# k of chunk 2 by 32x32 block loads and VectorE transposes, with the attention of chunks 2 to 5 placed 4 to 6 tiles later

## The chip, the cores and the metric

One core of a Trainium2 chip. The metric is the device time of one execution in microseconds (us). Lines such as L265 are lines of the kernel before; in the changed kernel the helpers stand at the same lines.

## The reference, cut to what matters

A decayed linear attention (a state of 64x64 a head) over 768 positions, then a feed-forward network with a tanh gelu.

```python
def _attn_ref(q, k, v):            # 4 batches, 8 heads, 768 positions, 64 wide
    gamma = 1.0 - 2.0 ** (-5.0 - np.arange(H))
    for t in range(S):
        state = gamma[None, :, None, None] * state + np.einsum('bhd,bhe->bhde', k[:, :, t], v[:, :, t])
        y[:, :, t] = scale * np.einsum('bhd,bhde->bhe', q[:, :, t], state)

def _moe_ref(x, w_in, w_out):      # 3072 tokens, 512 -> 2048 -> 512
    h = x @ w_in
    g = 0.5 * h * (1.0 + np.tanh(c * (h + 0.044715 * h * h * h)))
    return g @ w_out
```

## The kernel before

The positions are cut into six chunks of 128 (0 to 5). For each chunk c, M1 is `h = x @ w_in` with gelu and M2 is `g @ w_out`, 16 tiles each, on TensorE. The attention of chunk c+1 is strewn between those tiles: `att_T` gets q and k transposed, `att_AY` makes the score products A = k q (a pair of batches at a time), `att_Y` the outputs y, `att_S` the new state. TensorE's matmuls stand in the program's order, so the place of each piece is written down by tile number (a tile of 512 columns is four matmuls, 0.86 us).

A transposed operand comes in one of two ways. Either TensorE transposes it into PSUM and an engine copies it out, or it is loaded as 32x32 blocks, GpSimd scales it, and VectorE transposes the blocks within SBUF:

```python
    BLK = {"q": (2, 3, 4, 5), "k": (3, 4, 5)}       # the chunks that take the second way

    def load_blk(nm, c):                            # 16 DMAs of 64 KB, rows of 128 B
        t = ld_all((nm + ("32" if nm == "q" else "T32"), c))
        ...
                    nc.sync.dma_start(out=t[p0:p0 + 32, :, a, :], in_=src[j, dd, t0:t0 + 32])

    def mm_T(c, b):                                 # TensorE, into one of 4 "att" banks of PSUM
        parts = [(i, nm) for i, nm in enumerate("qk") if c not in BLK[nm]]
        ...
                nc.tensor.transpose(out=ps[:, i, hp], in_=pair(h16[nm, c, b], hp), identity=iden)

    def ev_T(c, b, eng=nc.vector):
        for i, nm in enumerate("qk"):
            if c in BLK[nm]:
                nc.vector.transpose(out=t[:, i]..., in_=blk16.pop((nm, c, b))...)
        if ("T", c, b) in pss:
            copy_on(eng, t[:, i0:], pss.pop(("T", c, b))[:, i0:])

    def att_AY(c, bs, tag, ca, abs_, eng):
        ...
        for b in abs_:
            mm_A(ca, b)                             # L265: 8 matmuls a batch, two "att" banks
        ...
            for b in abs_:
                ev_A(ca, b)                         # L278: VectorE, two instructions a batch
```

The schedule around M1 and M2 of chunk 1, and that of the later chunks (n is the next chunk; M1 has units 0 to 15, M2 has 16 to 31):

```python
    for b in range(B):
        load1(SY, "k", 2, b)                        # plain load of k, 256 KB
    load_blk("q", 2)
    ...                                             # three late output stores, v of chunk 2
    run(M1 of chunk 1, {...
            8: [(att_T, 2, 0), (load, 3)], 10: [(att_T, 2, 1)],
            13: [(att_AY, 2, (), "att", 2, (0, 1), None)],
            14: [(att_T, 2, 2)], 15: [(att_T, 2, 3)]})
    run(M2 of chunk 1, {1: [(att_AY, 2, (), "att", 2, (2, 3), None)], 4: [(att_Y, 2)], ...})
    for c in range(2, NCk - 1):
        after = {2: [prep q and k blocks], 6: [(att_T, n, 0)], 8: [(att_T, n, 1)] + [...],
            9: [(load, n + 1)], 10: [(att_T, n, 2)],
            12: [(att_AY, n, (), "att", n, (0, 1), None)], 14: [(att_T, n, 3)],
            17: [(att_AY, n, (), "att", n, (2, 3), None)], 21: [(att_Y, n)], 23 to 26: att_S}
```

## Time and profile before

| | kernel before |
|---|---|
| time, median of 3 runs | 213.74 us (213.71 to 213.85) |
| span of the profiled run | 212.4 us, granted clock 0.998 |
| TensorE busy | 97% |
| chain that ended last | 87% TensorE |
| DMA | 32.78 MB in 124289 packets, 118064 of them under 512 B |

TensorE is the bound nearly everywhere. The useful reading is by stage: from the first h_ps matmul of one chunk's M1 to that of the next one's. A stage holds M1 and M2 of one chunk with the attention of the next, and I name it after the attention in it ("the stage of chunk 3" is M1 and M2 of chunk 2). The lines on which the forecast rests stand in it below.

### The profile page before, as it was taken

The numbers are of one execution on the slowest core, as the hardware profiler recorded it, in microseconds if no ns is written. First come the engines' busy times: TensorE is split into PE (matmuls) and PEld (weight loads), VectorE is DVE, ScalarE is ACT, GpSimd is POOL, SyncE is SP. The second block draws the span as 40 slices with busy tenths as digits, with TensorE's granted clock in tenths as the row PEclk, the third lists the DMA queues.
The fourth block names the chain that finished last, engine by engine and source line by source line (L and its number), as shares of the span: only waits on it lengthen the run. The fifth ranks groups of instructions, "written<-read, shape, count | busy, mean of one in ns | idle before, by whom it ended". The sixth has DMA issues, their size and how long they took to land.

```text
span 212.4 us, 3868 instructions
## 1 busy us (share of the span) xinstructions
PE 205.6 (97%) x1516; PEld 111.3 (52%) x1516; DVE 89.2 (42%) x161; ACT 84.2 (40%) x141; POOL 95.8 (45%) x117
## 2 busy tenths in 40 slices
PE   7989999999999999999999999999999999999992
PEld 2457444457897564444464444464444464444461
DVE  5478201198619753365544365544355520100001
ACT  2374661255455131465131465131465131565110
POOL 2796400513819418599309599301599301100000
PEclk9999999999999999999999999999999999999999
DMA  6999999999789788979789996879910012100121
GB/s 157 288 250 207 206 203 233 241 241 231 127 222 224 112 161 159 252 177 175 120 162 190 303 192 103 124 153 241 281 34 3 0 49 102 49 0 0 49 92 59
DMA packets 124289, 32.78 MB, mean 154 GB/s; under 512 B 118064, under 2 KB 122416, under 8 KB 124272
## 3 DMA queue, kind: packets, MB, share of 16 engines
q1 hardware_dynamic: 108880, 20.75, 49.4%
q0 software_dynamic: 5600, 8.65, 17.2%
q10 hardware_dynamic: 9792, 3.15, 6.1%
q8 instruction: 12, 0.20, 0.4%
q14 instruction: 5, 0.04, 0.1%
HBM read 30.44 MB, written 6.29 MB: 173 GB/s over the span
## 4 chain that ended last, share of the span: by engine, by line
PE 87%; SPq 4%; DVE 2%; DMA 2%; ACT 1%; issue 1%; POOL 0%; POOLq 0%
PE o_ps L470 39%; PE h_ps L425 34%; SPq L110 4%; PE spin_ps L171 4%; PE a_ps L265 3%; PE y_ps L300 3%; PE y_ps L287 2%; DMA q<-in_q_dram 2%; PE s_ps L319 2%; PE qkT_ps L242 2%; ACT qkT L224 1%; DVE qkT L226 1%; DVE qkT L251 1%; POOL q L206 0%; DVE q L195 0%
## 5 line engine op out<-in xcount | busy, mean ns | idle before, releaser
L470 PE MATMUL o_ps<-w_out,g 128*128 128x512 f16 (+1 forms) x400 | 88.1, 371 | 0.0
L425 PE MATMUL h_ps<-xT,w_in 128*128 128x512 f16 (+1 forms) x464 | 86.8, 342 | 0.3 <-ACT g L440 0.2
L440 ACT ACTIVATE g<-h_ps 128x512 f16<-128x512 f32 x96 | 57.2, 597 | 47.8 <-PE h_ps L425 47.8
L425 PEld LDWEIGHTS <-w_in 128*128 128x128 f16 x464 | 44.4, 98 | 37.9 <-issue 0.3
L470 PEld LDWEIGHTS <-g 128*128 128x128 f16 x400 | 37.7, 98 | 38.8
L278 DVE TENSOR_TENSOR a_sb<-a_ps,mask 128x512 f16<-128x512 f32 x48 | 30.0, 682 | 15.9 <-PE a_ps L265 15.8
L492 ACT COPY o_sb<-o_ps 128x512 f32<-128x512 f32 x19 | 11.1, 586 | 54.3 <-PE o_ps L470 49.9
L497 POOL DMA_DIRECT2D out_dram<-o_sb x17 | 9.6, 564 | 46.9 <-ACT o_sb L492 35.0
L195 POOL TENSOR_TENSOR k<-k,cst 128x512 f16<-128x512 f32 x24 | 24.7, 1036 | 11.9 <-DMA k<-in_k_dram 11.8
L345 POOL TENSOR_TENSOR stg<-st,cst 128x512 f32<-128x512 f16 x16 | 16.3, 1041 | 11.5 <-DVE st L336 9.5
L206 POOL TENSOR_TENSOR q<-q,cst 128x512 f16<-128x512 f32 x16 | 16.6, 1048 | 5.2 <-DMA q<-in_q_dram 5.1
L336 DVE TENSOR_TENSOR st<-s_ps,stg 64x256 f16<-64x256 f32 x32 | 13.5, 422 | 7.8 <-PE s_ps L319 7.3
L251 DVE STREAM_TRANSPOSE qkT<-q 128x512 f16<-128x512 f16 x16 | 11.3, 706 | 11.7 <-POOL q L206 11.7
L195 DVE TENSOR_TENSOR q<-q,cst 128x512 f16<-128x512 f32 x8 | 6.3, 781 | 17.2 <-DMA q<-in_q_dram 17.2
L206 POOL TENSOR_TENSOR kT<-kT,cst 128x512 f16<-128x512 f32 x12 | 12.5, 1044 | 0.0
L226 DVE CAST xT<-y_ps 128x512 f16<-128x512 f32 x11 | 7.2, 686 | 11.9 <-PE y_ps L300 11.9
L508 DVE COPY o_sb<-o_ps 128x256 f32<-128x256 f32 x2 | 0.8, 424 | 26.6 <-PE o_ps L470 26.6
L224 ACT CAST xT<-y_ps 128x512 f16<-128x512 f32 x13 | 7.2, 588 | 9.9 <-PE y_ps L300 9.9
L171 PE MATMUL spin_ps<-zero 128*128 128x512 f16 x28 | 9.6, 499 | 1.3 <-DVE zero L139 1.3
L490 DVE COPY o_sb<-o_ps 128x512 f32<-128x512 f32 x4 | 2.8, 691 | 19.0 <-PE o_ps L470 14.7
L265 PE MATMUL a_ps<-qkT 64*128 64x128 f16 x192 | 8.3, 218 | 1.3 <-ACT qkT L224 0.7
L251 DVE STREAM_TRANSPOSE qkT<-kT 128x512 f16<-128x512 f16 x12 | 8.4, 700 | 2.6 <-POOL kT L206 2.6
(32 smaller groups left out, 98.2 us busy)
## 6 DMA issues: line engine op xcount, KB each, us to landing
v<-in_v_dram SPq DMA_DIRECT2D x22, 256.0 KB, 4.4
k<-in_k_dram SPq DMA_DIRECT2D x20, 256.0 KB, 4.9
out_dram<-o_sb POOLq DMA_DIRECT2D x17, 256.0 KB, 3.2
q<-in_q_dram SPq DMA_DIRECT2D x64, 64.0 KB, 2.7
kT<-in_k_dram SPq DMA_DIRECT2D x48, 64.0 KB, 2.7
w_out<-in_moe_w_out_dram POOLq DMA_DIRECT2D x4, 512.0 KB, 15.5
w_in<-in_moe_w_in_dram POOLq DMA_DIRECT2D x3, 512.0 KB, 8.9
q<-in_q_dram SPq DMA_DIRECT2D x5, 256.0 KB, 6.1
```

Source lines behind the costliest of these rows:

```text
L171: nc.tensor.matmul(out=ps, lhsT=zero[:, 0:128], rhs=zero, start=True, stop=True)
L195: eng.tensor_tensor(out=t, in0=src, in1=cst[:, col:col + H].unsqueeze(2).broadcast_to([128, H, Dh]), op=ALU.mult,)
L206: nc.gpsimd.tensor_tensor(out=t, in0=ld_all((key, c))[:, b * NHP:(b + 1) * NHP].rearrange("p hp a d -> p (hp a) d"), in1=cst[:, col:col + ...
L251: nc.vector.transpose(out=t[:, i].rearrange("p hp t -> p (hp t)"), in_=blk16.pop((nm, c, b)).rearrange("p ha d -> p (ha d)"),)
L265: nc.tensor.matmul(out=ps[j][:, hp], lhsT=t[j * 64:(j + 1) * 64, 1, hp], rhs=t[j * 64:(j + 1) * 64, 0, hp], start=True, stop=True,)
L278: nc.vector.tensor_tensor(out=s, in0=ps[j], in1=mask[:, j], op=ALU.mult)
L336: eng.tensor_tensor(out=st[sl, :, b, sl], in0=s_ps[sl, :, sl], in1=stg[sl, :, b, sl], op=ALU.add,)
L345: nc.gpsimd.tensor_tensor(out=stg[:, :, b], in0=st[:, :, b], in1=cst[:, OG:OG + NHP].unsqueeze(2).broadcast_to([128, NHP, 128]), op=ALU.mult,)
L425: nc.tensor.matmul(out=out, lhsT=w_in_of(fc, kc), rhs=xT[c][:, kc, t0:t1], start=(kc == 0 and first), stop=(kc == NHP - 1), skip_group_che ...
L440: nc.scalar.activation(out=out, in_=in_, func=AF.Gelu_apprx_tanh, scale=1.0)
L470: nc.tensor.matmul(out=ps[:, n0:n1], lhsT=g_sb[c, fc // 2][:, fc % 2, b * C:(b + 1) * C], rhs=w_out_sb[fc // (NF // NO)][:, fc % (NF // NO ...
L492: nc.scalar.copy(out=o_sb, in_=ps)
```

## The change

Its intent: k of chunk 2 also takes the block way, so TensorE loses 16 transposes of 128x128. Since these blocks arrive later, the attention moves back in all later stages. Plain k is still loaded, as the state product needs it.

```diff
-    BLK = {"q": (2, 3, 4, 5), "k": (3, 4, 5)}
+    BLK = {"q": (2, 3, 4, 5), "k": (2, 3, 4, 5)}
...
-    for b in range(B):
-        load1(SY, "k", 2, b)
     load_blk("q", 2)
+    load_blk("k", 2)
     for rows, o_sb in late: ...
-    (v of chunk 2; preps of k, q, v of chunk 2 at once)
+    (v, then k of chunk 2); load(3); prep(2, "Q")
...  M1 of chunk 1
-            8: [(att_T, 2, 0), (load, 3)], 10: [(att_T, 2, 1)],
-            13: [(att_AY, 2, (), "att", 2, (0, 1), None)],
-            14: [(att_T, 2, 2)], 15: [(att_T, 2, 3)],
+            7: [(prep, 2, "Kvk")],
...  M2 of chunk 1
-            1: [(att_AY, 2, (), "att", 2, (2, 3), None)], 4: [(att_Y, 2)], 6 to 9: att_S
+            1: [(att_T, 2, 0), (att_T, 2, 1)],
+            3: [(att_AY, 2, (), "att", 2, (0, 1), None), (att_T, 2, 2), (att_T, 2, 3)],
+            7: [(att_AY, 2, (), "att", 2, (2, 3), None)], 11: [(att_Y, 2)], 12 to 15: att_S
...  chunks 3 to 5
+            2: [(prep, n, "QKvk")],
-            6: T0, 8: T1, 10: T2, 12: A(0,1), 14: T3, 17: A(2,3), 21: Y, 23 to 26: S
+            14: T0, T1, 17: A(0,1), T2, T3, 22: A(2,3), 26: Y, 27 to 30: S
```

(The last two lines are shortened; T, A, Y and S stand for att_T, att_AY, att_Y and att_S.)

More of the change, by code (lines that the diff above doesn't have):

```diff
@@ L634, with prep @@
     )
-    for b in range(B):
-        load1(SY, "k", 2, b)
     load_blk("q", 2)
+    load_blk("k", 2)
     for rows, o_sb in late:
         nc.sync.dma_start(out=rows, in_=o_sb)
-    for b in range(B):
-        load1(SY, "v", 2, b)
-    for nm in "kqv":
+    for nm in "vk":
         for b in range(B):
-            prep_blk("q", 2, b) if nm == "q" else prep1(PO, nm, 2, b)
+            load1(SY, nm, 2, b)
+    load(3)
+    def prep(c, nms):
+        for nm in nms:
+            for b in range(B):
+                prep1(PO, nm, c, b) if nm in "kv" else prep_blk(nm.lower(), c, b)
+    prep(2, "Q")
     run(
@@ L657 @@
             6: [(att_S, 1, 3)],
-            8: [(att_T, 2, 0), (load, 3)],
-            10: [(att_T, 2, 1)],
-            13: [(att_AY, 2, (), "att", 2, (0, 1), None)],
-            14: [(att_T, 2, 2)],
-            15: [(att_T, 2, 3)],
+            7: [(prep, 2, "Kvk")],
         },
@@ L667 @@
         {
-            1: [(att_AY, 2, (), "att", 2, (2, 3), None)],
-            4: [(att_Y, 2)],
-            6: [(att_S, 2, 0)],
-            7: [(att_S, 2, 1)],
-            8: [(att_S, 2, 2)],
-            9: [(att_S, 2, 3)],
+            1: [(att_T, 2, 0), (att_T, 2, 1)],
+            3: [(att_AY, 2, (), "att", 2, (0, 1), None), (att_T, 2, 2), (att_T, 2, 3)],
+            7: [(att_AY, 2, (), "att", 2, (2, 3), None)],
+            11: [(att_Y, 2)],
+            12: [(att_S, 2, 0)],
+            13: [(att_S, 2, 1)],
+            14: [(att_S, 2, 2)],
+            15: [(att_S, 2, 3)],
         },
@@ L680 @@
         after = {
-            2: [(prep_blk, nm, n, b) for b in range(B) for nm in "qk"],
-            6: [(att_T, n, 0)],
-            8: [(att_T, n, 1)] + [(prep1, PO, nm, n, b) for b in range(B) for nm in "kv"],
+            2: [(prep, n, "QKvk")],
             9: [(load, n + 1)] if n + 1 < NCk else [],
-            10: [(att_T, n, 2)],
-            12: [(att_AY, n, (), "att", n, (0, 1), None)],
-            14: [(att_T, n, 3)],
-            17: [(att_AY, n, (), "att", n, (2, 3), None)],
-            21: [(att_Y, n)],
-            23: [(att_S, n, 0)],
-            24: [(att_S, n, 1)],
-            25: [(att_S, n, 2)],
-            26: [(att_S, n, 3)],
+            14: [(att_T, n, 0), (att_T, n, 1)],
+            17: [(att_AY, n, (), "att", n, (0, 1), None), (att_T, n, 2), (att_T, n, 3)],
+            22: [(att_AY, n, (), "att", n, (2, 3), None)],
+            26: [(att_Y, n)],
+            27: [(att_S, n, 0)],
+            28: [(att_S, n, 1)],
+            29: [(att_S, n, 2)],
+            30: [(att_S, n, 3)],
         }
```

## The prediction

> **What bounds the kernel now.** I read the share of each engine first, then the chain that ended last, then the timelines of single engines in the two kinds of stage that the change touches. The page's first part:
>
> ```profile
> PE 205.6 (97%) x1516; PEld 111.3 (52%) x1516; DVE 89.2 (42%) x161; ACT 84.2 (40%) x141; POOL 95.8 (45%) x117
> ```
>
> TensorE is busy for 97% of a 212.4 us span (the timed median, 213.74 us, is 1.3 us more), and the chain is 87% TensorE. Of the 6.8 us without a matmul, about 1.3 lie before the first and 3.8 after the last. So only two things can move the time: matmul work taken off TensorE, and waits of TensorE in the middle. The view of TensorE's waits holds only one of those in the part that the change touches, 0.30 us at 66 us. It is the end of this chain (start, us, what):
>
> ```profile
> 58.22 0.49 SPq L110
> 58.70 0.04 issue
> 58.75 3.79 DMA q<-in_q_dram
> ...
> 62.93 1.06 POOL q L206
> 63.99 0.02 issue
> 64.02 0.72 DVE qkT L251
> 64.74 0.02 issue
> 64.76 0.42 DVE qkT L226
> 65.18 0.62 DVE qkT L251
> 65.80 0.32 DVE qkT L226
> 66.12 0.05 issue
> 66.17 0.40 PE a_ps L265 x8
> 66.56 0.98 PE h_ps L425 x8
> 67.54 0.22 PE qkT_ps L242 x4
> ```
>
> The q blocks of chunk 2 land at 62.54, GpSimd scales them, VectorE transposes them, and the A product of the second batch (L265) stands until 66.17. Eight such matmuls take 0.33 us where nothing is missing; the first of the pair began at 65.47, so 0.37 us is lost. The last line is one of four groups of k transposes, 0.22 us each.
>
> In chunks 3 to 5 there is no such wait: the times from one chunk's first h_ps to the next one's are 31.86, 31.85 and 30.96 us (the last stage has no state products), all TensorE.
>
> **What the Trainium skill says.** "TensorE: Matmul & The Clock Gate", Part 4, gives about 275 to 390 ns for a 128x128 transpose and says that the result goes to PSUM and needs a copy. The copy agrees (L226, 0.38 to 0.42 us); the time doesn't apply here: in a stream four take 0.22 us, 56 ns each, and I use that. "VectorE: DVE Perf Modes", The three transpose paths, says that VectorE transposes 32x32 blocks only, which is why k has to arrive as blocks; in the trace one of 128x512 takes 0.70 us. "DMA: Bandwidth & Descriptors", Specifications, asks for 512 B or more a transfer for line rate; the block loads move 128 B rows, and agree: 64 KB each 0.53 us, 124 GB/s. "SBUF — State Buffer", Who interferes with whom, says that a VectorE instruction with one SBUF input doesn't contend with GpSimd outside the two-port modes; transposes last 0.71 us beside busy GpSimd, so I add nothing for the longer GpSimd work.
>
> **The change, part by part.** *Removed:* 16 transposes of k on TensorE, 4 x 0.22 = 0.9 us on the bound engine, and the four 0.4 us copies on VectorE. *Added:* four VectorE transposes of 0.70 (net +1.2 us), four GpSimd scalings of 1.04 (+4.2 us) and 16 DMAs of 64 KB, since k is still loaded plainly too. All of that lies beside TensorE; in itself it costs nothing. *Moved:* the q wait of 0.37 us goes, as q now heads the queue. So the change is worth -1.26 us if the new order makes no waits.
>
> I find two places where it does. First, arrival. The DMA queue of before:
>
> ```profile
> 44.87 3.66 SPq L98 DMA_DIRECT2D k<-in_k_dram  x4
> 48.62 10.62 SPq L110 DMA_DIRECT2D q<-in_q_dram  x16
> 59.33 2.31 SPq L641 DMA_DIRECT2D out_dram<-o_sb  x3
> ```
>
> In the new order the q blocks start at 44.9, end 10.6 later at 55.5, and the k blocks follow, 9.5 us (their time for chunk 3 in before): 65.0. The last lands 2.8 to 3.8 later, at 67.8 to 68.8. GpSimd can then scale batch 0 and 1 (2 x 1.04, plus 0.3 for its wait on eight semaphores), VectorE ends the second transpose 0.75 after that: 70.9 to 71.9. When does TensorE ask? The last half of M1 loses the four k groups (0.9) and the first A pair with its wait (1.03), so M2 of chunk 1 starts at 68.70 - 1.93 = 66.77, not 68.70. The pair of A products stands after four tiles of 0.864: batch 0 at 70.2, batch 1 at 70.5. Batch 1 waits 0.4 to 1.4, I take 0.9 us.
>
> Second, VectorE between the A pairs. The program order that I built has, on VectorE: four evictions of A(0,1), then all four transposes of batches 2 and 3, then A(2,3) on TensorE. In before only one batch's transposes stood behind the evictions. VectorE, then TensorE, of chunk 3 in before:
>
> ```profile
> 97.83 2.48 DVE L278 TENSOR_TENSOR a_sb<-a_ps,mask 128x512 f16<-128x512 f32 x4 [3.13 <-PE a_ps L265]
> 100.23 0.70 DVE L251 STREAM_TRANSPOSE qkT<-q 128x512 f16<-128x512 f16 x1
> 100.86 0.67 DVE L251 STREAM_TRANSPOSE qkT<-kT 128x512 f16<-128x512 f16 x1
> ```
>
> ```profile
> 97.40 0.62 PE L265 MATMUL a_ps<-qkT 64*128 64x128 f16 x16
> 97.95 2.76 PE L425 MATMUL h_ps<-xT,w_in 128*128 128x512 f16 x12
> 100.55 1.89 PE L470 MATMUL o_ps<-w_out,g 128*128 128x512 f16 x8
> 102.38 0.62 PE L265 MATMUL a_ps<-qkT 64*128 64x128 f16 x16
> ```
>
> From the start of the first pair, evictions begin after 0.43 and take 2.40; the transposes start 0.63 apart, so four end at 0.43 + 2.40 + 3 x 0.63 + 0.70 = 5.42. Batch 3 is asked for after five tiles between the pairs, which is 4.98, plus 0.28 for batch 2: 5.26. With the hand-over of 0.05 that is a wait of 0.2 us in each of chunks 3, 4 and 5: 0.6. For chunk 2 only four tiles lie between the pairs: 4.98 - 0.86 + 0.28 = 4.4 against 5.47. If batch 1 waited there, A and evictions shift together and 1.0 remains.
>
> Sum: -0.9 - 0.37 + 0.9 + 1.0 + 0.6 = +1.2 us, which makes 214.9.
>
> The rest I checked for room and let stand. kT16 has two buffers, so GpSimd's scaling of batches 2 and 3 waits for the first two transposes, but they come before the evictions in VectorE's order. Chunk 2's v and k land by 79, while the first state product is asked for at about 82.7. The next chunk's blocks arrive some 8 us later than before, k's of chunk 3 at 95.5 and scaled by 99.8, and its first A pair now stands at about 102.
>
> **The rivals.** *All gain, no wait:* the k blocks land by 67 and VectorE's order is quick enough; then -1.3, 212.5 us. For it: arrivals are an estimate from durations under other traffic, and 0.2 us in chunks 3 to 5 is within its error. Against: in chunk 2 the 1.0 us needs VectorE alone, whatever the DMA does. *The queue becomes the bound:* it carries 9.5 us more in a stretch in which it stood almost without pause from 41 to 130 us, and every later chunk's blocks come late. Against: a chunk's loads take 28 to 30 us with their waits, of its 31.85, and the moved tiles give 3.5 to 7 us back; for: each late microsecond at an A pair goes straight to the end, so k landing 2 us later than I think makes 217. *GpSimd becomes the bound:* its 16 scalings of about 15.5 us plus decays of 4 fit a chunk of 31.85; output stores stand behind the scalings in its order, which could hold the output buffers, four of them. I expect nothing of it.
>
> **Range and chances.** If k arrives just in time and the small waits vanish, -0.2; the DMA 1.5 us later than taken and double waits in chunks 3 to 5, near +2.8. So 213.4 to 216.6, 214.9 in the middle. Two per cent is 4.3 us: a gain of that size would need more than the whole that can be taken off, a loss would need the late queue. Faster 0.01, same 0.94, slower 0.05.
>
> **What would show it.** Of the new profile: 16 fewer matmuls and no L242 row for k of chunk 2; M2 of chunk 1 begins near 66.8 us, from 68.7; k blocks land at 67.8 to 68.8; idle of TensorE at L265 of 0.4 to 1.4 us near 70.5 and about 1.0 us near 75, both released by VectorE's transpose; three idles of about 0.2 us, one in each of chunks 3 to 5, at the second A pair, with a chunk of about 32.05 us. The prediction is wrong if the pair near 75 doesn't wait, if waits stand at y_ps or s_ps, which I gave none, or if chunks 3 to 5 lengthen by more than 0.5 us each.

## The result, and the profile after

| | before | changed |
|---|---|---|
| median | 213.73 us (213.60 to 213.85, 4 runs) | 214.62 us (214.15 to 214.99, 4 runs) |
| ratio | | 1.0041, 95% interval 1.0016 to 1.0065 |
| span of the profiled run | 212.4 us | 213.2 us |
| granted clock | 0.998 | 1.000 |
| packets | 124289 | 132737 |

A ratio is taken over fast runs as the record gives it, and is not quite the ratio of the medians quoted. The changed kernel is 0.4% slower, 0.9 us; by the mark of 2% used here that counts as the same.

By stage, from the starts of the first h_ps matmul in the timeline of TensorE (before: 50.58, 86.08, 117.93, 149.79, 180.75; changed: 50.07, 85.26, 118.39, 150.41, 181.54):

| stage | before | changed | difference | forecast |
|---|---|---|---|---|
| chunk 2 | 35.50 | 35.19 | -0.31 | +0.6 |
| chunk 3 | 31.85 | 33.13 | +1.28 | +0.2 |
| chunk 4 | 31.86 | 32.02 | +0.16 | +0.2 |
| chunk 5 | 30.96 | 31.13 | +0.17 | +0.2 |
| the rest, to the end | 31.65 | 31.66 | 0.0 | 0 |

The sum is +1.3 us; 0.5 comes off because M1 of chunk 1 began half a microsecond sooner in this execution (50.07 instead of 50.58), which the change can't reach. The first part of the page says that TensorE has 16 matmuls less:

```profile
PE 204.9 (96%) x1500; PEld 110.2 (52%) x1500; DVE 89.8 (42%) x161; ACT 84.2 (40%) x141; POOL 100.2 (47%) x121
```

The timeline of TensorE in the changed kernel (start, us, engine, line, what, and in brackets the idle before it with its releaser). Chunk 2's two pairs, chunk 3's first pair, chunk 4's second:

```profile
69.71 0.88 PE L265 MATMUL a_ps<-qkT 64*128 64x128 f16 x16
70.53 3.63 PE L470 MATMUL o_ps<-w_out,g 128*128 128x512 f16 x16
74.09 0.40 PE L265 MATMUL a_ps<-qkT 64*128 64x128 f16 x8
75.11 0.40 PE L265 MATMUL a_ps<-qkT 64*128 64x128 f16 x8 [0.62 <-DVE qkT L251]
75.44 3.63 PE L470 MATMUL o_ps<-w_out,g 128*128 128x512 f16 x16
...
101.21 0.40 PE L265 MATMUL a_ps<-qkT 64*128 64x128 f16 x8 [0.24 <-DVE qkT L251]
102.39 0.40 PE L265 MATMUL a_ps<-qkT 64*128 64x128 f16 x8 [0.79 <-DVE qkT L251]
102.72 4.49 PE L470 MATMUL o_ps<-w_out,g 128*128 128x512 f16 x20
...
139.00 0.79 PE L265 MATMUL a_ps<-qkT 64*128 64x128 f16 x16
139.72 3.63 PE L470 MATMUL o_ps<-w_out,g 128*128 128x512 f16 x16
```

A pair without a wait takes 0.55 us from its start to the next tile. Here chunk 2's first pair takes 0.82 (70.53 - 69.71), a loss of 0.27, and the second 1.35, a loss of 0.80. Chunk 4's second pair takes 0.72: 0.17 lost, too short for a bracket. Chunk 3's first pair is the large one, 1.27 us lost: where it doesn't wait, it begins 15.63 us after the stage does (134.02 - 118.39, the first pair of chunk 4 in this same run), which is 100.89, and should hand over at 101.45 instead of 102.72, with the pair's 0.55 us.

What it waits for is k of chunk 3. The DMA queue of the changed kernel:

```profile
55.87 9.21 SPq L110 DMA_DIRECT2D kT<-in_k_dram  x16
65.17 1.41 SPq L640 DMA_DIRECT2D out_dram<-o_sb  x3
66.63 4.59 SPq L98 DMA_DIRECT2D v<-in_v_dram  x4
71.28 4.12 SPq L98 DMA_DIRECT2D k<-in_k_dram  x4
75.49 11.26 SPq L110 DMA_DIRECT2D q<-in_q_dram  x16
86.86 9.84 SPq L110 DMA_DIRECT2D kT<-in_k_dram  x16
```

The first line is what the change adds. The last is chunk 3's k, issued up to 96.7 us; in the kernel before the same 16 DMAs began at 75.07 and ended at 84.5. GpSimd starts to scale them at 99.36, and two batches with their transposes take it to 102.34:

```profile
99.36 4.11 POOL L206 TENSOR_TENSOR kT<-kT,cst 128x512 f16<-128x512 f32 x4 [5.62 <-DMA kT<-in_k_dram]
```

GpSimd stood idle for 5.62 us until these DMAs landed, so it is not GpSimd that made them late.

### The profile page after: what moved, and what is told of

It is laid out like the page before. It is cut to its first block, busy times and chain, and to the rows that moved or that the text cites. A ratio compares the mean times of both kernels' runs of the same rounds, so it can differ in the third digit from the quotient of the medians.

```text
span 213.2 us, 3846 instructions
## 1 busy us (share of the span) xinstructions
PE 204.9 (96%) x1500; PEld 110.2 (52%) x1500; DVE 89.8 (42%) x161; ACT 84.2 (40%) x141; POOL 100.2 (47%) x121
## 2 busy tenths in 40 slices
DMA packets 132737, 33.82 MB, mean 159 GB/s; under 512 B 126512, under 2 KB 130864, under 8 KB 132720
## 4 chain that ended last, share of the span: by engine, by line
PE 76%; SPq 9%; DMA 7%; DVE 3%; issue 2%; POOL 1%; ACT 0%; POOLq 0%; DVEq 0%
PE o_ps L470 34%; PE h_ps L425 33%; SPq L110 8%; DMA k<-in_k_dram 3%; DMA w_in<-in_moe_w_in_dram 3%; PE a_ps L265 2%; PE y_ps L300 2%; DVE qkT L251 2%; PE s_ps L319 2%; PE y_ps L287 2%; DVE a_sb L278 2%; DMA kT<-in_k_dram 1%; PE qkT_ps L242 1%; SPq L98 0%; POOL kT L206 0%
## 5 line engine op out<-in xcount | busy, mean ns | idle before, releaser
L425 PE MATMUL h_ps<-xT,w_in 128*128 128x512 f16 (+1 forms) x464 | 85.6, 342 | 0.4 <-ACT g L440 0.2
L251 DVE STREAM_TRANSPOSE qkT<-kT 128x512 f16<-128x512 f16 x16 | 10.9, 679 | 26.3 <-POOL kT L206 26.3
L206 POOL TENSOR_TENSOR kT<-kT,cst 128x512 f16<-128x512 f32 x16 | 16.4, 1045 | 11.3 <-DMA kT<-in_k_dram 8.8
L195 DVE TENSOR_TENSOR q<-q,cst 128x512 f16<-128x512 f32 x8 | 7.3, 916 | 17.9 <-DMA q<-in_q_dram 17.9
L192 POOL CAST v<-v 128x512 f16<-128x512 f32 x16 | 9.4, 613 | 4.8 <-DMA v<-in_v_dram 4.8
L265 PE MATMUL a_ps<-qkT 64*128 64x128 f16 x192 | 9.0, 218 | 2.5 <-DVE qkT L251 1.7
L265 PEld LDWEIGHTS <-qkT 64*128 64x128 f16 x192 | 5.4, 94 | 9.2 <-DVE qkT L251 5.2
```

Source lines behind the costliest of these rows:

```text
L195: eng.tensor_tensor(out=t, in0=src, in1=cst[:, col:col + H].unsqueeze(2).broadcast_to([128, H, Dh]), op=ALU.mult,)
L206: nc.gpsimd.tensor_tensor(out=t, in0=ld_all((key, c))[:, b * NHP:(b + 1) * NHP].rearrange("p hp a d -> p (hp a) d"), in1=cst[:, col:col + ...
L251: nc.vector.transpose(out=t[:, i].rearrange("p hp t -> p (hp t)"), in_=blk16.pop((nm, c, b)).rearrange("p ha d -> p (ha d)"),)
L265: nc.tensor.matmul(out=ps[j][:, hp], lhsT=t[j * 64:(j + 1) * 64, 1, hp], rhs=t[j * 64:(j + 1) * 64, 0, hp], start=True, stop=True,)
L425: nc.tensor.matmul(out=out, lhsT=w_in_of(fc, kc), rhs=xT[c][:, kc, t0:t1], start=(kc == 0 and first), stop=(kc == NHP - 1), skip_group_che ...
```

## The experiments

All stages in one table, in us, as above. The lines of the experiments are read against it.

| run | chunk 2 | chunk 3 | chunk 4 | chunk 5 |
|---|---|---|---|---|
| before | 35.50 | 31.85 | 31.86 | 30.96 |
| changed | 35.19 | 33.13 | 32.02 | 31.13 |
| order_only | 36.01 | 32.02 | 32.02 | 31.13 |
| split_pair | 34.85 | 33.62 | 32.07 | 31.17 |
| late3 | 35.36 | 32.09 | 32.02 | 31.13 |
| split_late3 | 34.35 | 32.07 | 32.07 | 31.17 |
| best | 34.13 | 31.86 | 31.85 | 30.96 |
| t2_early | 35.16 | 31.85 | 31.86 | 30.96 |
| block_only | 40.87 | 31.85 | 31.86 | 30.96 |
| queue_only | 35.67 | 38.21 | 31.85 | 30.96 |
| after_again | 35.17 | 33.07 | 32.03 | 31.13 |
| t2_again | 35.16 | 33.14 | 31.85 | 30.96 |

Times scatter: on the chips of these runs the fast runs of the kernel before differ by 1.1 to 1.6 us, and those of two other kernels by about 3 us, so many ratios below have intervals as wide as the effects. The stages of one profile are sharper, where a wait is what differs. Runs named slow were left out of the ratios. All results were correct.

The first four ran on one chip with the kernel before at a median of 214.44 us over 11 runs, one of them slow.

### order_only: the new places without the blocks

```diff
-    BLK = {..., "k": (2, 3, 4, 5)}
+    BLK = {..., "k": (3, 4, 5)}
-    load_blk("q", 2); load_blk("k", 2); late stores; v, k of chunk 2
+    k of chunk 2; load_blk("q", 2); late stores; v of chunk 2
```

> The new order of the attention alone: k of chunk 2 loads plainly and TensorE transposes it, as in the kernel before, and the loads stand in the order of before. Theory (two waits: the second A pair waits for VectorE, and the first pair of chunk 3 waits for k blocks that come late because the queue carries 16 more DMAs): without the extra DMAs the k blocks of chunk 3 land near 87 us, so the first pair of chunk 3 doesn't wait and that stage takes 32.0 us instead of 33.13; chunk 2 keeps its transposes (0.9 us) and loses the q wait (0.37); chunks 3 to 5 keep 0.17 each: about 213.9 us in all. Rival (the order itself makes the wait in chunk 3, whatever is in the queue): the wait of about 1 us at the first pair of chunk 3 stays, and the time is about 215.

Measured: 215.08 us, ratio 1.0034 (1.0013 to 1.0055). Chunk 3's stage is 32.02, as the theory said and not the rival: with 16 DMAs fewer in the queue the same places don't wait there. The total is 0.7 us over the kernel before by the ratio, where I had expected 0.2, by waits that I had overlooked, in chunk 2:

```profile
70.30 0.62 PE L265 MATMUL a_ps<-qkT 64*128 64x128 f16 x16
71.47 0.38 PE L242 MATMUL qkT_ps<-iden,k 128*128 128x128 f16 x4 [0.56 <-DVE a_sb L278]
72.07 0.38 PE L242 MATMUL qkT_ps<-iden,k 128*128 128x128 f16 x4 [0.22 <-DVE a_sb L278]
```

The A pair has just taken all four "att" banks of PSUM, and the transposes of batches 2 and 3, now right behind it, need one each, which comes free when VectorE has evicted. So these new places, in this order, only suit an operand that needs no PSUM: the two parts of the change belong together.

### split_pair: the second pair of A products apart and later

```diff
-            7: [(att_AY, 2, (), "att", 2, (2, 3), None)],
+            8: [(att_AY, 2, (), "att", 2, (2,), None)],
+            9: [(att_AY, 2, (), "att", 2, (3,), None)],
-            22: [(att_AY, n, (), "att", n, (2, 3), None)],
+            22: [(att_AY, n, (), "att", n, (2,), None)],
+            23: [(att_AY, n, (), "att", n, (3,), None)],
```

> The changed kernel with A of batches 2 and 3 no longer as a pair: batch 2 a tile later and batch 3 two tiles later in chunk 2, batch 3 one tile later in chunks 3 to 5. Theory: the waits at the second pair (0.8 us in chunk 2, 0.17 in chunks 4 and 5) go. But the arrival of chunk 3's k blocks is set by the queue and not by TensorE, so TensorE reaches the first pair of chunk 3 0.8 us sooner and waits 0.8 us longer there, 1.8 instead of 1.0: only about 0.35 us comes off the end, 214.3 us. Rival (waits of TensorE add up, each one worth its length): 214.62 - 0.8 - 0.34 = 213.5.

Measured: 215.15 us, ratio 1.0038 (1.0010 to 1.0067), five runs and a slow one. The waits at the second pair went, and still nothing was gained. Chunk 3's first pair is why, in this run:

```profile
101.23 0.40 PE L265 MATMUL a_ps<-qkT 64*128 64x128 f16 x8 [0.52 <-DVE qkT L251]
102.42 0.40 PE L265 MATMUL a_ps<-qkT 64*128 64x128 f16 x8 [0.79 <-DVE qkT L251]
```

The second batch starts at 102.42, against 102.39 in the changed kernel, though TensorE came there sooner: the last k block was issued at 96.4 us, against 96.7, so the arrival is fixed by the queue. The stage of chunk 3 got 0.49 longer as that of chunk 2 got 0.34 shorter. Chunk 2 fell by less than the 0.8 expected, since the first pair lost 0.51 here (69.80 to 70.86, with a bracket of 0.34 in the same view) where the changed kernel lost 0.27, and since the split has a cost. That cost is the one thing that was wrong: chunks 4 and 5 are no shorter, 32.07 and 31.17. There is no idle bracket left at A in them. In chunk 4 the tiles stop at 139.24 and 140.54 for a group of 8 each, and go on 0.33 us later; a group of 16 takes 0.55. The four matmuls between the two groups take 0.97 from start to start instead of 0.86, so there is also 0.1 us of loss ahead of a group. Two groups instead of one cost 0.2 us, what the wait had cost.

### late3: chunk 3 alone two tiles later

```diff
+        if n == 3:
+            after = {i + (2 if 14 <= i <= 22 or i == 23 else 1 if i > 23 else 0): v for i, v in after.items()}
```

> The changed kernel with the attention of chunk 3 alone two tiles (1.73 us) later. Theory: the wait of 1.03 us at the first pair of chunk 3 goes, the second pair then waits 0.17 as in chunks 4 and 5: 213.75 us, and the stage of chunk 3 takes 32.0 to 32.3 us. Rival (the k blocks of chunk 3 come later when they are asked for later, the queue being held by waits for buffers): the wait stays at half or more, 214.2 or over.

Measured: 214.22 us, ratio 1.0005 (0.9976 to 1.0034). The stage of chunk 3 is 32.09, from 33.13: of the 1.27 us at its first pair, 0.23 are left (it began at 102.75 and handed over at 103.53), and they are not put off to the second pair. The time alone couldn't have told it from the kernel before.

### split_late3: both edits

> Both edits. Theory: 0.8 in chunk 2, 1.0 in chunk 3 and 0.17 in each of chunks 4 and 5 go, with 0.1 left in chunk 3 as TensorE comes there 0.8 us sooner than in the run with late attention alone: 212.5 us, faster than the kernel before by about 1.2 (the 0.9 of the transposes and the 0.37 of the q wait). More than the sum of what the two edits give singly. Rival (waits add up): the two gains singly measured, added.

Measured: 213.71 us, ratio 0.998 (0.9951 to 1.0010). In the profile the two gains add to more than they give singly, as expected: chunk 2 is 34.35, chunk 3 32.07 with no idle bracket, where split_pair alone had 33.62. The stages of chunk 2 and 3 together are 66.42 us, against 68.32 in the changed kernel, 68.47 with split_pair and 67.45 with late3. The times can't prove more than the sum: 1.0038, 1.0005 and 0.998 have intervals of about 0.003 each way. It fell short of the 1.2 us: the four stages are 0.51 us shorter than those of the kernel before, and those of best, below, which doesn't split, 1.37. The difference of 0.86 is four times the 0.2 us of the split groups.

### best, t2_early: one batch instead of two behind the evictions

```diff
-            14: [(att_T, n, 0), (att_T, n, 1)],
-            17: [(att_AY, n, (), "att", n, (0, 1), None), (att_T, n, 2), (att_T, n, 3)],
+            14: [(att_T, n, 0), (att_T, n, 1), (att_T, n, 2)],
+            17: [(att_AY, n, (), "att", n, (0, 1), None), (att_T, n, 3)],
```

That is the whole of t2_early. The kernel best has in addition chunk 2's second pair at tile 9 instead of 7, unsplit, and chunk 3's transposes two tiles and its first pair three tiles later (16 and 20; second pair 25, Y 28, states 29 to 31). These two and the next two ran on one chip, with the kernel before at 213.69 us over 11 runs.

> The changed kernel with three moves and nothing taken away: in chunk 2 the second A pair two tiles later (kept as a pair, since the runs with single A groups showed about 0.2 us more for two groups than for one pair), in chunk 3 the first pair three tiles later, in chunks 3 to 5 the transposes of batch 2 ahead of the evictions of the first pair, as in the kernel before. Theory: no wait of TensorE is left but up to 0.4 us at the arrival of chunk 2's k blocks. From the start of M1 of chunk 1 the stages take 34.3 to 34.6, 31.85, 31.85 and 30.96 us, 0.9 to 1.2 less in all than in the kernel before: a ratio of 0.9945 to 0.996. Rival (the remainder is a cost of the late order that no wait explains): stages of 32.0 in chunks 3 and 4, a ratio of 0.998 or more.

Measured: 212.24 us, ratio 0.994 (0.9920 to 0.9959), six runs. The stages of chunks 3 to 5 are those of the kernel before, and chunk 2's is 1.37 us shorter, at 34.13 a little better than the 34.3 expected. No wait at A is left:

```profile
69.77 0.62 PE L265 MATMUL a_ps<-qkT 64*128 64x128 f16 x16
75.61 0.62 PE L265 MATMUL a_ps<-qkT 64*128 64x128 f16 x16
...
102.49 0.62 PE L265 MATMUL a_ps<-qkT 64*128 64x128 f16 x16
```

This is the gain that the change was after: 0.6% below the kernel before, clear of noise but under the 2% mark. The changed kernel was not run on this chip; against the kernel before it stood at 1.0041 and 1.0017, so best is ahead of it too.

> The changed kernel with one edit in chunks 3 to 5: VectorE transposes batch 2 before the evictions of the first pair, so that one batch instead of two stands between the evictions and the second pair. Theory (the 0.17 us a chunk are the wait for the transposes of batch 3): the stages of chunks 4 and 5 go from 32.02 and 31.13 back to 31.85 and 30.96; chunk 3 keeps its wait for the k blocks, 33.1; about 0.35 us in all. Rival (they are a cost of the place, say of A beside M2 tiles): both stages stay at 32.02 and 31.13.

Measured: 213.49 us, ratio 0.9993 (0.9975 to 1.0012). Chunks 4 and 5 are back at 31.86 and 30.96, so the 0.17 us were the wait for the fourth batch's transposes, and the rival is out. But chunk 3's wait, which this edit should not touch, was gone too. That needed an explanation, and so the two runs at the end.

### block_only and queue_only: what the move is for

block_only has the blocks at the old places; queue_only is the kernel before and 16 loads more that nobody reads.

```diff
 (block_only, against the kernel before)
+    BLK = {..., "k": (2, 3, 4, 5)}; loads in the order of the changed kernel
+            7: [(prep_blk, "k", 2, b) for b in range(B)] + [(prep1, PO, nm, 2, b) for nm in "vk" for b in range(B)],
 (queue_only, against the kernel before)
     (v of chunk 2)
+    load_blk("k", 2)
-                bufs=2 if key[0] == "q32" else 1,
+                bufs=2,
```

> The k blocks of chunk 2 without the move: attention at the places of the kernel before. Theory (the blocks arrive when the queue has carried q's 16 and k's 16, near 67 us, which the places of before can't wait for): the first pair of chunk 2 is asked for at 65.0 and waits about 4.7 us, the second 1.3, chunk 3's pairs 0.3 to 1 each: about 220 us. Rival (the move was not needed, and the changed kernel's time is all made by the move): about 213 to 214 us.

Measured: 219.06 us, ratio 1.0250 (1.0224 to 1.0277), four fast runs. The two batches of chunk 2's first pair waited 3.20 and 0.58 us, less than the 4.7 I had said, and the second pair and chunk 3's pairs, for which I had 1.3 and 0.3 to 1, not visibly; yet the stage is 5.37 us longer. The reason stands in the view by stretches (after the bounds and the length: busy time of TensorE, its weight loads, VectorE, ScalarE and GpSimd, then the granted clock, the DMA share and GB/s):

```profile
58.40:64.70 6.30, 6.30 (x60) 5.43 (x57) 1.56 (x3) 4.18 (x7) 4.69 (x5) 1.00 0.74 115
64.70:69.60 4.90, 1.12 (x17) 0.69 (x16) 2.42 (x4) 0.60 (x1) 3.53 (x4) 0.79 1.06 274
69.60:73.30 3.70, 3.70 (x21) 2.56 (x18) 3.70 (x8) 0.62 (x2) 2.89 (x5) 0.50 1.05 236
```

The granted clock fell to 0.50 at 67.5 us, 2.8 us into the first wait, and stayed there until 74.3 (finer stretches of the same view). After the wait 16 h_ps matmuls took 3.38 us from start to start instead of 1.75. So this wait was paid a second time.

> The kernel before, and nothing of the change but 16 DMAs of 64 KB of k blocks of chunk 2 that nobody reads (a wrong use of bandwidth on purpose; the result stays right), ahead of chunk 3's loads, into a buffer of their own. Theory (the queue alone makes chunk 3's blocks late): chunk 2's stage stays at 35.5, k of chunk 3 lands 9.5 us later, near 96.7, the first pair of chunk 3 waits about 2.9 us, the second about 1.0: some 217.7 us. Rival (the bandwidth is there, the transfers are hidden): within 0.3 us of the kernel before.

Measured: 219.53 us, ratio 1.0269 (1.0222 to 1.0316), four fast runs. Nothing in it differs but the loads and their buffer, and the first pair of chunk 3 waits 1.53 us for its first batch and 1.61 for its second (expected: 2.9 in all; the second pair, for which I had 1.0, doesn't wait). The clock falls here too (0.50 from 100.1 to 106.9 us), and 12 h_ps matmuls take 5.10 us instead of 2.60. So the transfers are not hidden: at the old places, 1 MB more in the queue costs 2.7%. Chunk 2's stage stays within 0.2.

### after_again, t2_again: how much the queue's pace differs

The changed kernel and t2_early once more, together on a third chip, where the kernel before had 214.43 us over 11 fast runs.

> The changed kernel once more, for its scatter. The run with batch 2 transposed early had no wait at chunk 3's first pair, and its k blocks were issued 2 us sooner than in the first profile of the changed kernel (94.6 instead of 96.7 us for the last), with no edit that could move them. If the queue's pace differs from run to run, then this profile shows the first pair of chunk 3 waiting 0 to 1.1 us according to the time at which k's last block is issued: no wait if that is before about 95.2, about 1 us if it is 96.7. If the early transposes did it, this profile has the wait of 1 us again and k's last block at 96 to 97 us.

> The kernel with batch 2 transposed early once more, beside the changed kernel on the same chip. Both show the same wait at chunk 3's first pair if their last k blocks are issued at the same time; the stages of chunks 4 and 5 are 31.85 and 30.96 here, 32.02 and 31.13 there.

Measured: 215.06 us, ratio 1.0017 (0.9994 to 1.0041), and 215.16 us, ratio 1.0043 (1.0002 to 1.0084). Chunk 3's k blocks in t2_early, then in after_again, then in t2_again:

```profile
84.81 9.81 SPq L110 DMA_DIRECT2D kT<-in_k_dram  x16
```

```profile
86.98 9.40 SPq L110 DMA_DIRECT2D kT<-in_k_dram  x16
```

```profile
87.28 9.25 SPq L110 DMA_DIRECT2D kT<-in_k_dram  x16
```

Last issue at 94.6, 96.4 and 96.5 us, and stages of 31.85, 33.07 and 33.14. The run after_again alone could not decide, as its outcome fits both the queue's pace and the early transposes. t2_again decides: the same edit has the wait in one execution and not in the other, as the queue runs; with the changed kernel's first profile (96.7; 33.13) and best (95.6, but asked later, at 102.49) that is one rule: chunk 3 waits when its k is late. That chunks 4 and 5 differ between the two kernels by 0.18 and 0.17, side by side on one chip, is the second effect again. The overall ratios can't show it: their intervals overlap.

## Why the prediction was right, point by point

The forecast was 214.9 us, the median is 214.62, and the direction and the two kinds of wait are the ones named. Its terms are less good than their sum, which owes something to luck.

- **Removed, 0.9 + 0.37 us.** Held, a little low: best, in which no wait at A is left, is 1.37 us shorter in chunk 2's stage. The transposes and scalings that came in cost nothing by themselves, as forecast. The 0.1 us more is the q wait, which was sized too small. In the kernel before the first pair of chunk 2 stood like this, with the next tile at 66.50:

```profile
65.47 0.40 PE L265 MATMUL a_ps<-qkT 64*128 64x128 f16 x8
66.17 0.40 PE L265 MATMUL a_ps<-qkT 64*128 64x128 f16 x8 [0.30 <-DVE qkT L226]
```

  That is 1.03 us from start to next tile, against 0.55 for a pair without a wait: 0.48 lost, where the forecast took only the pause between the two groups. 0.90 + 0.48 makes 1.38.
- **"Batch 1 waits 0.4 to 1.4, I take 0.9 us."** Too large. The first pair of chunk 2 lost 0.27 us, and nothing in t2_early, after_again and t2_again (0.55 us from start to next tile). The issue of k's blocks ended at 65.1, as worked out (65.0), but GpSimd began to scale at 67.16, so they had landed within 2.1 us of the last issue, not 2.8 to 3.8. The larger figure was q's landing in the kernel before.
- **VectorE between the pairs, 1.0 us in chunk 2.** Shown, 0.80. Where the first pair lost nothing (the same three runs) the second lost 0.97, so the size was right. What failed is "If batch 1 waited there, A and evictions shift together and 1.0 remains": with a wait at the first pair the second lost 0.17 less. So a small one hardly shows in chunk 2's stage (35.19 us, against 35.16 to 35.17 in those three), a larger one does (0.44 lost and 35.36 in late3). A wait of that kind (brackets of 0.62 to 0.79) is there in every run with k's blocks and the pair at tile 7, and gone in those with the pair later.
- **0.2 us in each of chunks 3 to 5.** Shown for 4 and 5: 0.16 and 0.17, which t2_early takes away. In chunk 3 no such wait appeared: the first pair stood torn apart by its own wait, so that VectorE began the evictions (102.37) 0.35 us ahead of the tiles that follow the pair (102.72), and the second pair found its transposes done.
- **"k's of chunk 3 at 95.5 and scaled by 99.8, and its first A pair now stands at about 102."** This step failed at both ends. Scaling began at 99.36, 3.9 us later than 95.5. In the queue the plain loads took 8.7 us, against 7.1 in the kernel before, and q's blocks 11.3 against 9.8. And the pair was asked for at 100.9, 1.1 us before the 102, as chunk 2's stage came out 0.9 us shorter than forecast and M1 of chunk 1 had begun 0.5 sooner. So a place that I had checked and called safe lost 1.27 us, the largest wait of the changed kernel. The rival "the queue becomes the bound" had the mechanism, and order_only, late3 and queue_only show it; I gave it to the tail and it was in the middle.
- The total came out by luck: +1.1 forgotten in chunk 3 stood against 0.6 too much at chunk 2's first pair, 0.2 too much at its second, and 0.1 too little removed; and that profile began its M1 of chunk 1 half a microsecond sooner, which no step had.
- Of the signs of being wrong: the pair near 75 us did wait, and there were no waits at y_ps or s_ps. "If chunks 3 to 5 lengthen by more than 0.5 us each" came true for chunk 3 alone (1.28).

So the 1.4 us that the change takes off TensorE were lost again to three waits: VectorE's order between the pairs of A (0.8 to 1.0 in chunk 2, 0.17 twice later), k's arrival in chunk 2 (0 to 0.5), and k's arrival in chunk 3 (0 to 1.3, as the queue runs). Later places take away the first in chunk 2 and the third, an earlier transpose of batch 2 takes away the 0.17, and then the gain is there: 212.24 against 213.69 us. For the second nothing was done: in best the blocks of chunk 2 came in time by themselves.

What stays open: why the queue's pace differs by 2 us at 95 us between executions. Most of it, 1.6 us, is already there where the loads of chunk 3's q begin (73.90 us in t2_early, 75.49 in the changed kernel).

## What to carry to other kernels

Work taken off a busy engine counts only when every operand that now takes another way still arrives in time. Where a queue runs almost without pause, work out the arrival of the *next* loads behind the ones that you add, not only of those, and allow for a pace that differs by a few per cent. A wait for a fixed arrival swallows gains made ahead of it (split_pair), so take the last wait away first or all of them together; and judge edits of a few tenths of a microsecond by the length of the stage in a profile, not by the time of the whole.

## What the Trainium skill lacked or had wrong

- "TensorE: Matmul & The Clock Gate", Part 4: its 275 to 390 ns for a 128x128 transpose are not what one costs between other matmuls. Four take 0.22 us from start to start, 56 ns each, and the 16 removed gave 0.9 of the 1.37 us.
- The same page, Why this matters for your kernels, warns of gaps above about 3 us between matmuls. The runs agree roughly (the granted clock fell to 0.50 2.8 us into a wait of 3.20 us), but show the same in the second of two waits of 1.53 and 1.61 us with eight small matmuls between them, 2.9 us after the first began: in these runs one unbroken gap of 3 us was not needed. Another section of that page, on depth-cycling of the PSUM queue, does tell of a clock lost by frequent short idles, but gives no lengths.
- No page has a time for going over to a group of 64-row matmuls amid 128-row ones and back ("TensorEngine Tiling (Array Packing)", Key Properties, says only that changing the tiling mode drains TensorE; that this is the cause here was not tested). Two groups of 8 instead of one of 16 took about 0.2 us a chunk more (stages of 32.07 with no idle bracket, against 31.85).
- "DMA: Bandwidth & Descriptors" gives a fixed cost and a bandwidth, but nothing on how much the pace of a full queue scatters. The same sequence of loads reached its last k block of chunk 3 at 94.6 to 96.7 us in four executions, and a kernel placed to the microsecond loses or gains 1.3 us by it.
